# Loads on two queues and four tiles transposed on TensorE, at the start of a gated attention and SwiGLU kernel

## The chip, the cores and the metric

The kernel runs on one core of a Trainium2 chip. The metric is the device time of one execution in microseconds (us). All runs here are in the undisturbed ("fast") state. The profile calls the engines PE (TensorE), DVE (VectorE), ACT (ScalarE), POOL (GpSimd) and SP (SyncE, which issues most loads).

## The reference

The input x has 2048 tokens of 512 features, in bf16. One branch is a linear attention with 32 heads, the other a SwiGLU block; a sigmoid gate mixes them.

```python
x = A_x                                              # 1 x 2048 x 512
g = sigmoid((x * gate_w).sum(-1, keepdims=True))
q, k, v = split(x @ wqkv)                            # (cut)
pq, pk = phi(q), phi(k)         # phi(t) = where(t > 0, t + 1, exp(t)) + 1e-6
o = pq @ (pk^T v) / (pq . sum(pk) + 1e-6)            # for each head
a = o @ wo
b = (silu(x @ w1) * (x @ w3)) @ w2
return g * a + (1 - g) * b
```

## The kernel before

Only the first 10 us matter here. A tile of x is 128 tokens, and there are 16 of them. The k projection needs each tile transposed (xT, features on partitions) and the weights wk. Tiles 0 and 1 are loaded plainly and transposed on PE through an identity matmul; tiles 2 and 3 and all later ones are transposed by DMA. Everything is loaded through the one queue of the sync engine, in the order written.

```python
nc.scalar.activation(out=pre[:], ..., func=ACT.Exp)        # loads ACT's function table early
dq = nc.sync
dq.dma_start(out=x_sb[:, 0:1, :], in_=x_r[:, 0:1, :])      # x tile 0
for i in range(2):                                         # wk in two halves
    dq.dma_start(out=wk_sb[:, 2*i:2*i+2, :], ...)
dq.dma_start(out=x_sb[:, 1:2, :], in_=x_r[:, 1:2, :])      # x tile 1
dq.dma_start(out=xT[:, :, 2*P:TB], in_=x2d[2*P:TB, :], transpose=True)   # tiles 2, 3
dq.dma_start(out=x_sb[:, 2:TPB, :], in_=x_r[:, 2:TPB, :])
# ... tiles 4 to 15 (a DMA transpose and a plain load for each four), then the other weights

def emit_xT(t):                              # one tile: four transposes, one copy from PSUM
    for kc in range(KC):
        nc.tensor.transpose(out=xTp[:, kc, :], in_=x_sb[:, t, kc*P:(kc+1)*P], identity=ident[:])
    if t in (0, 2): nc.vector.tensor_copy(out=xT_t, in_=xTp[:])
    else:           nc.scalar.activation(out=xT_t, in_=xTp[:], func=ACT.Copy)

emit_warm(6)                                 # matmuls on constants
emit_xT(0)
emit_warm(2)
emit_k_mm(k0[0], 0, 0); emit_k_mm(k0[0], 0, 1)     # k(0), first half of wk
emit_xT(1)
emit_k_mm(k0[0], 0, 2); emit_k_mm(k0[0], 0, 3)     # k(0), second half of wk
emit_k_phi(k0[0], 0)                         # exp on ACT, two operations on DVE
for t in range(1, TPB):                      # k(1), k(2), k(3)
    ...
# then, alternating: "XP" matmuls (x^T phi(k)) of tile u and k(t) for t = 4 to 15
```

In the code P is 128, TB is the 512 tokens of a block of TPB = 4 tiles, and KC = 4 counts the chunks of 128 features. k(t) is the projection of tile t, and k(0,2..3) are the last two of its four matmuls. The order of PE's instructions is the written one. The order on the other engines is chosen by the scheduler.

## Time and profile before

The time is 181.27 us (three runs, 181.25 to 181.48). The profiled execution spans 179.2 us.

| reading | value |
|---|---|
| PE busy | 174.8 us, 98% of the span |
| begin of the XP matmuls in the chain | 9.36 us |
| gap before tile 1's transposes, from the end of the matmul slot before it | 0.52 us |
| gap before k(1), likewise | 0.42 us |

First, the page of before. The line is PE's busy time, its share of the span, and its number of instructions.

```profile
PE 174.8 (98%) x884; PEld 83.7 (47%) x884; DVE 118.0 (66%) x202; ACT 65.8 (37%) x123; POOL 61.4 (34%) x69
```

Second, the table of PE's waits in before: the waiting group, what it waited for, the total in us, how often, the longest. These three lines are the whole table. After the first k tiles PE waits no more, so what matters is when the XP matmuls begin.

```profile
PE warm L159 <- PEq L462: 0.8, 1, 0.8
PE xTp L168 <- DMA x_sb<-in_A_x_dram: 0.4, 1, 0.4
PE k L178 <- ACT xT L175: 0.3, 1, 0.3
```

Third, the chain of waits of before in the first 16 us: start, duration, what.

```profile
2.23 3.24 DMA x_sb<-in_A_x_dram
...
5.51 0.41 PE xTp L168 x4
...
5.95 0.60 ACT xT L175
...
6.60 2.76 PE k L178 x12
9.36 0.86 PE XP L198 x4
```

Tile 1 is issued at 2.23 us, behind wk, and lands at 5.465. Then ACT's copy of its transpose (0.60 us) holds k(1) until 6.60.

Fourth, the timeline of PE in before: start, duration of the group, line, operation, tiles, count.

```profile
0.84 2.72 PE L159 MATMUL warm<-const-bfloat16-1.0 128*128 128x512 bf16 x6 [0.84 <-PEq L462]
3.35 0.63 PE L168 MATMUL xTp<-ident,x_sb 128*128 128x128 bf16 x4
3.78 0.95 PE L159 MATMUL warm<-const-bfloat16-1.0 128*128 128x512 bf16 x2
4.56 0.59 PE L178 MATMUL k<-wk_sb,xT 128*128 128x512 bf16 x2
5.51 0.40 PE L168 MATMUL xTp<-ident,x_sb 128*128 128x128 bf16 x4 [0.35 <-DMA x_sb<-in_A_x_dram]
```

The last matmul of a group shows its whole latency, 0.38 us, while matmuls follow each other every 0.216 us; so the wait "0.35" counts from the modelled end, and the time that PE's slot stood empty is larger: the second k(0) matmul starts at 4.78, its slot ends at 4.99, and the transposes start at 5.51, which is 0.52 us. In the same way the gap before k(1) is 6.60 less 6.18, or 0.42 us.

### The profile page before, as it was taken

To read this page: it belongs to the slowest core of one execution; us is meant where nothing else is said; L and a number is where in the kernel's file an instruction comes from. 1 tells how busy PE (TensorE), PEld (TensorE's weight loads), DVE (VectorE), ACT (ScalarE), POOL (GpSimd) and SP (SyncE) were. 2 spreads that over 40 slices of the span, in tenths; PEclk is the share of its full clock that TensorE was granted. 3 is DMA by queue.
4 is the path that set the end of the run, shared out by engine and by line. 5 is a ranking of instruction groups with operands and counts; after the bars stand their busy time and mean duration, and the time that the engine had idled before them with its cause. 6 is when DMAs were issued, how large, how long until landed. Compare 5 with 4: busy or idle time off the path is not lost.

```text
span 179.2 us, 2463 instructions
## 1 busy us (share of the span) xinstructions
PE 174.8 (98%) x884; PEld 83.7 (47%) x884; DVE 118.0 (66%) x202; ACT 65.8 (37%) x123; POOL 61.4 (34%) x69
## 2 busy tenths in 40 slices
PE   8899999999999999999999999999999999999993
PEld 3344444474444545444445444444545444444463
DVE  1388667897998837398787374977764669776000
ACT  3442322566523334343324343332443323331221
POOL 5177765646453323253003232620032328100000
PEclk9999999999999999999999999999999999999999
DMA  5999999901006011115000101240001013300011
GB/s 165 244 242 239 294 334 398 348 28 26 9 11 110 0 44 33 44 42 104 0 0 4 44 31 42 59 90 5 0 7 54 19 59 67 61 0 0 29 46 45
DMA packets 29340, 15.14 MB, mean 84 GB/s; under 512 B 20656, under 2 KB 28304, under 8 KB 29328
## 3 DMA queue, kind: packets, MB, share of 16 engines
q1 hardware_dynamic: 29328, 14.98, 31.2%
q8 instruction: 7, 0.11, 0.3%
q14 instruction: 5, 0.04, 0.1%
HBM read 8.42 MB, written 2.10 MB: 59 GB/s over the span
## 4 chain that ended last, share of the span: by engine, by line
PE 93%; DVE 2%; DMA 2%; SPq 1%; ACT 0%; issue 0%; DVEq 0%
PE o_ps L344 19%; PE gate_ps L301 18%; PE up_ps L307 18%; PE o_ps L335 8%; PE q_ps L211 8%; PE XP L198 8%; PE k_ps L178 6%; PE r_ps L235 3%; PE o_ps L339 2%; DMA x_sb<-in_A_x_dram 2%; PE k L178 2%; DVE hT L317 1%; DVE gs L314 1%; PE kvT_ps L402 0%; SPq L86 0%; PE W_ps L429 0%
## 5 line engine op out<-in xcount | busy, mean ns | idle before, releaser
L301 PE MATMUL gate_ps<-xT,w_sb 128*128 128x512 bf16 x160 | 41.1, 379 | 0.0
L307 PE MATMUL up_ps<-xT,w_sb 128*128 128x512 bf16 x160 | 41.1, 379 | 0.0
L219 POOL TENSOR_TENSOR qz<-pq,z_sb 128x512 f32<-128x512 bf16 x16 | 18.5, 1162 | 60.2 <-DVE pq L143 58.6
L312 ACT ACTIVATE th<-gate_ps 128x512 bf16<-128x512 f32 x40 | 23.9, 597 | 38.2 <-PE gate_ps L301 37.8
L344 PE MATMUL o_ps<-w_sb,hT 128*128 128x512 bf16 (+2 forms) x180 | 37.5, 355 | 0.0
L314 DVE SCALAR_TENSOR_TENSOR gs<-th,gate_ps 128x512 bf16<-128x512 bf16 x40 | 27.3, 682 | 5.9 <-ACT th L312 5.6
L317 DVE TENSOR_TENSOR hT<-up_ps,gs 128x512 bf16<-128x512 f32 x40 | 27.7, 691 | 3.8
L140 DVE TENSOR_SCALAR phi_m<-phi_e 128x512 bf16<-128x512 bf16 x32 | 14.4, 450 | 23.0 <-ACT phi_e L138 22.9
L344 PEld LDWEIGHTS <-hT 128*128 128x128 bf16 x180 | 16.8, 97 | 17.9
L307 PEld LDWEIGHTS <-w_sb 128*128 128x128 bf16 x160 | 15.6, 98 | 19.0 <-issue 0.2
L301 PEld LDWEIGHTS <-w_sb 128*128 128x128 bf16 x160 | 15.6, 98 | 18.9 <-issue 0.3
L349 ACT ACTIVATE o_out<-o_ps,omg 128x512 bf16<-128x512 f32 (+2 forms) x17 | 11.1, 656 | 30.4 <-PE o_ps L344 30.4
L284 POOL TENSOR_TENSOR pqn<-pq,rden 128x512 bf16<-128x512 bf16 x16 | 16.6, 1056 | 14.1 <-DVE rden L277 11.7
L188 POOL TENSOR_TENSOR pks<-pks,pk_sb 128x512 f32<-128x512 f32 x15 | 17.6, 1173 | 8.9 <-DVE pk_sb L143 8.4
L222 DVE TENSOR_REDUCE den<-qz 128x32 f32<-128x512 f32 x16 | 10.9, 684 | 8.9 <-POOL qz L219 8.8
L335 PE MATMUL o_ps<-W_sb,pqT 128*128 128x512 bf16 (+2 forms) x72 | 16.8, 355 | 0.0
L211 PE MATMUL q_ps<-wq_sb,xT 128*128 128x512 bf16 x64 | 16.3, 379 | 0.0
L198 PE MATMUL XP<-pk_sb,x_sb 128*128 128x512 bf16 x64 | 16.1, 379 | 0.0
L138 ACT ACTIVATE phi_e<-k_ps 128x512 bf16<-128x512 f32 x12 | 7.2, 597 | 15.3 <-PE k_ps L178 15.3
L178 PE MATMUL k_ps<-wk_sb,xT 128*128 128x512 bf16 x48 | 12.3, 379 | 0.0
L138 ACT ACTIVATE phi_e<-q_ps 128x512 bf16<-128x512 f32 x16 | 9.6, 597 | 7.0 <-PE q_ps L211 6.8
L143 DVE SCALAR_TENSOR_TENSOR pq<-q_ps,phi_m 128x512 bf16<-128x512 f32 x16 | 11.1, 691 | 0.5
(59 smaller groups left out, 116.5 us busy)
## 6 DMA issues: line engine op xcount, KB each, us to landing
w_sb<-in_B_w_dram SPq DMA_DIRECT2D x3, 1280.0 KB, 9.6
out_dram<-o_out SPq DMA_DIRECT2D x15, 128.0 KB, 1.9
x_sb<-in_A_x_dram SPq DMA_DIRECT2D x3, 512.0 KB, 4.3
wk_sb<-in_A_wqkv_dram SPq DMA_DIRECT2D x2, 256.0 KB, 3.0
wq_sb<-in_A_wqkv_dram SPq DMA_DIRECT2D x1, 512.0 KB, 4.9
wv_sb<-in_A_wqkv_dram SPq DMA_DIRECT2D x1, 512.0 KB, 6.6
wo_sb<-in_A_wo_dram SPq DMA_DIRECT2D x1, 512.0 KB, 10.5
x_sb<-in_A_x_dram SPq DMA_DIRECT2D x2, 128.0 KB, 2.7
```

The lines of the kernel that those rows point to most:

```text
L178: nc.tensor.matmul(k_ps[:], lhsT=xT[:, kc, t * P : (t + 1) * P], rhs=wk_sb[:, kc, :], start=(kc == 0), stop=(kc == KC - 1),)
L188: nc.gpsimd.tensor_add(pks[:], pks[:], pk_sb[:, t, :])
L198: nc.tensor.matmul(XP_ps[dc][:], lhsT=x_sb[:, t, dc * P : (dc + 1) * P], rhs=pk_sb[:, t, :], start=(t == 0), stop=(t == NT - 1),)
L211: nc.tensor.matmul(q_ps[:], lhsT=xT[:, kc, ts_tok], rhs=wq_sb[:, kc, :], start=(kc == 0), stop=(kc == KC - 1),)
L219: nc.gpsimd.tensor_tensor(out=qz[:], in0=st[tb, "pq"][:, tt, :], in1=z_sb[:], op=ALU.mult)
L301: nc.tensor.matmul(gate_ps[:], lhsT=w1_sb[:, kc, fsl], rhs=xT[:, kc, tok_sl], start=(kc == 0), stop=(kc == KC - 1),)
L307: nc.tensor.matmul(up_ps[:], lhsT=w3_sb[:, kc, fsl], rhs=xT[:, kc, tok_sl], start=(kc == 0), stop=(kc == KC - 1),)
L312: nc.scalar.activation(out=th[:], in_=gate_ps[:], func=ACT.Tanh, scale=0.5)
L314: nc.vector.scalar_tensor_tensor(out=gs[:], in0=th[:], scalar=1.0, in1=gate_ps[:], op0=ALU.add, op1=ALU.mult)
L317: nc.vector.tensor_tensor(out=st[tb, "hT"][:, fc, :], in0=up_ps[:], in1=gs[:], op=ALU.mult)
L335: nc.tensor.matmul(o_ps[:], lhsT=st[tb, "pqT"][:, c, tsl], rhs=W_sb[:, c, a:b], start=(c == 0), stop=False,)
L344: nc.tensor.matmul(o_ps[:], lhsT=st[tb, "hT"][:, fc, tsl], rhs=w2_sb[:, fc, a:b], start=False, stop=(fc == FC - 1),)
```

## The change

The intent is to start k earlier. wk is issued from ACT's queue beside x tile 0 on the sync queue, so tile 1 is not behind it. Tiles 2 and 3 are also transposed on PE, so their DMA transpose is gone. Each transposed tile leaves PSUM in two halves, one by DVE and one by ACT.

```diff
-    pre = consts.tile([1, 1], FP32, name="pre")
-    nc.scalar.activation(out=pre[:], ..., func=ACT.Exp)
     dq.dma_start(out=x_sb[:, 0:1, :], in_=x_r[:, 0:1, :])
     for i in range(2):
         kcs = slice(2 * i, 2 * i + 2)
-        dq.dma_start(out=wk_sb[:, kcs, :], in_=wqkv_r[:, kcs, D : 2 * D])
+        nc.scalar.dma_start(out=wk_sb[:, kcs, :], in_=wqkv_r[:, kcs, D : 2 * D])
     dq.dma_start(out=x_sb[:, 1:2, :], in_=x_r[:, 1:2, :])
-    dq.dma_start(out=xT[:, :, 2 * P : TB], in_=x2d[2 * P : TB, :], transpose=True)
     dq.dma_start(out=x_sb[:, 2:TPB, :], in_=x_r[:, 2:TPB, :])
+    pre = consts.tile([1, 1], FP32, name="pre")
+    nc.scalar.activation(out=pre[:], ..., func=ACT.Exp)
 # ... emit_xT:
-        xTp = psX.tile([P, KC, P], BF16, tag=f"XP{t % 3}", name="xTp")
-        ... four transposes; tiles 0, 2 copied by DVE, the others by ACT
+        for h in range(2):
+            xTp = psX.tile([P, 2, P], BF16, tag=f"XP{(2 * t + h) % 3}", name="xTp")
+            ... two transposes
+            if h == 0: nc.vector.tensor_copy(out=xT_t, in_=xTp[:])
+            else:      nc.scalar.activation(out=xT_t, in_=xTp[:], func=ACT.Copy)
 # ... PE's order:
     emit_k_phi(k0[0], 0)
+    emit_xT(2)
     for t in range(1, TPB):
         ... k(t)
+        if t == 1:
+            emit_xT(3)
```

## The prediction

> **What bounds the kernel.** TensorE. The page's busy table gives PE 174.8 us of a 179.2 us span (98%); the chain of waits is 93% PE. The table of waits has only three PE waits in the whole run: 0.8 us at the start, 0.4 us for x tile 1, and 0.3 us for the ScalarE copy of that tile's transpose. So after the first k tiles PE never waits, and the time is the moment at which the "XP" matmuls begin (9.36 us in the chain) plus a fixed PE-bound rest. The change can only move that moment.
>
> **The start of before (timeline, chain).** Six warm-up matmuls hold PE until 3.35 us; x tile 0 lands earlier, at 2.95. Four transposes, two more warm-ups and the DVE copy (0.42 us) bring k(0) to 4.56. x tile 1 is issued only at 2.23, behind x0 and both halves of wk, and lands at 5.47: PE idles 0.35 us. Transposes at 5.51, then k(0,2..3) at 5.75; the ACT copy (0.60 us) makes PE wait again until 6.60. Twelve matmuls then take 2.76 us.
>
> **Removed.** The DMA transpose of tiles 2 and 3 (1.32 us of issue on the sync queue). Everything behind it there is issued some 2.2 us earlier (1.32 plus wk's two issues, 0.42 and 0.46). The wait for x1: now issued near 1.25, I expect it landed by about 4.5, before PE wants it (4.98). The wait for the 0.60 us ACT copy: two halves on two engines, about 0.27 us on DVE and 0.4 on ACT (estimates: about half of 0.42; between the 0.20 of the 1x1 activation and 0.60).
>
> **Added.** Eight transposes on PE at full clock. Before, four took 5.51 to 5.75, so eight cost about 0.5 us, on the critical path. Four half copies each on DVE and ACT in all, instead of one whole one each. The ACT table load (1.28 us) slides to about 1.7 to 3.0, still before ACT's first copy.
>
> **DMA.** The Trainium skill ("DMA: Bandwidth & Descriptors", Issuing engines are not separate DMA queues) says the queues share the same engines and a second issuer saves only issue time. The DMA row agrees that data soon limits: 0.87 to 1.14 busy from 3 to 6 us. So wk beside x0 may delay x0 by up to 0.35 us (harmless: the warm-ups end at 3.35), and wk's second half, now sharing with tiles 2 and 3, should land near 5.2 to 5.5 and gate k(0,2).
>
> **Sum.** k(0) still starts at 4.56 (warm-ups). x1 transposes at 4.98; k(0,2..3) end near 5.65 to 5.95 (6.18 before). Then xT(2), k(1), xT(3), k(2), k(3): 0.25 + 0.86 + 0.25 + 1.72 = 3.08 us, to 8.75 to 9.05. Gain 0.3 to 0.6 us, if no evacuation stalls PE. The risk is DVE order: if the copy of tile 2 queues behind phi(0) (exp 0.59, then 0.29 and 0.69), and tile 3's behind phi(1), PE stalls about 1.3 us and the change loses 0.7 to 1.0 us. Before's GpSimd timeline shows the scheduler taking ready work out of written order (blockmask memset between the two ident steps), so I think this the less likely case, about one in three.
>
> **Prediction: 180.9 us, range 180.3 to 182.0.** Faster by over 2%: 0.01; within 2%: 0.98; slower by over 2%: 0.01.
>
> **What shows it right.** No PE wait for x1; k(0) still near 4.56; the chain reaching "XP" between 8.7 and 9.1; PE's busy time unchanged or up 0.5 us; nothing new waiting later.
>
> **What makes it wrong.** Half copies behind phi on DVE (PE waits on "xT" near 7 to 9 us); wk or tiles 2 and 3 landing after 6 us; a late table load.

## The result, and the profile after

The changed kernel took 181.20 us (four runs, 180.65 to 181.62) against 181.38 us (four runs, 181.25 to 181.73). The ratio is 0.9985, 95% interval 0.9962 to 1.0009: the same. Here and below a ratio is the mean time of one kernel's fast runs over that of the other's of the same rounds, so it is not quite the ratio of the medians quoted. The changed kernel's four runs lie 1.0 us apart, the others 0.5.

The profiled execution is one of the slower ones (181.62 us, span 179.9). Its page, the same line as before: PE is 1.2 us busier.

```profile
PE 176.0 (98%) x892; PEld 84.7 (47%) x892; DVE 118.9 (66%) x205; ACT 66.7 (37%) x126; POOL 61.2 (34%) x69
```

PE's table of waits after has one line. Both waits that the change aimed at are gone.

```profile
PE warm L158 <- PEq L466: 0.8, 1, 0.8
```

The chain of waits after, first 16 us. It is all PE from the start, yet XP begins 0.47 us later than in the trace of before.

```profile
0.84 2.72 PE warm L158 x6
3.56 0.43 PE xTp L169 x4
3.98 0.85 PE warm L158 x2
4.84 0.85 PE k L179 x2
5.69 0.43 PE xTp L169 x4
6.12 0.68 PE k L179 x2
6.80 0.22 PE xTp L169 x4
7.02 0.86 PE k L179 x4
7.88 0.22 PE xTp L169 x4
8.11 1.73 PE k L179 x8
9.83 0.86 PE XP L199 x4
```

The timeline of PE after shows why. The same two k(0) matmuls take 1.06 us (0.59 before), and the same four transposes of tile 1 take 0.63 us (0.40 before).

```profile
3.78 1.06 PE L158 MATMUL warm<-const-bfloat16-1.0 128*128 128x512 bf16 x2
4.63 1.06 PE L179 MATMUL k<-wk_sb,xT 128*128 128x512 bf16 x2
5.49 0.63 PE L169 MATMUL xTp<-ident,x_sb 128*128 128x128 bf16 x4
5.91 0.88 PE L179 MATMUL k<-wk_sb,xT 128*128 128x512 bf16 x2
6.63 0.39 PE L169 MATMUL xTp<-ident,x_sb 128*128 128x128 bf16 x4
```

PE ran at half its clock until about 6.5 us here, and until about 4.5 us in the trace of before. The traces hold records of the clock that agree with the matmuls' pace: before is released to full clock at 4.49 us, after at 6.49. What PE does up to 4.4 us is the same instruction for instruction, so the change did not cause the later release. The page's row of granted clock does not show any of it: it prints 9 in the first slices of both, because there is no record ahead of the first release. At the start of a kernel the spacing of equal matmuls is the safer reading.

The Trainium skill, "TensorE: Matmul & The Clock Gate" (The HAM clock gate), says that PE starts at half clock, and that a monitor with a free-running window of 3.413 us releases it, at a moment that varies from run to run. These traces agree: in all ten traces of kernels of this length the full clock then lasts 174.08 us, which is 51 windows of 3.413.

The loads did what was expected of them. My reading of the trace's landing records: tile 1 landed at 4.21 us (5.46 before), wk's halves at 3.85 and 4.97 (4.07 and 4.83), tiles 2 and 3 at 5.88.

The two theories taken to the chip:

- A, the clock: the change does gain 0.3 to 0.6 us where the clock is released early; with a late release the wait that it removes was not there, and a kernel that never waits takes on the whole variation of the release.
- B, refill: the eight added transposes, and the landing of tiles 2 and 3, use up what the removed waits gave, and the rest is the noise of the chip.

### The profile page after: what moved, and what is told of

The parts are those of the page before. It is cut to its first block, busy times and chain, and to the rows that moved or that the text cites. A ratio compares the mean times of both kernels' runs of the same rounds, so it can differ in the third digit from the quotient of the medians.

```text
span 179.9 us, 2484 instructions
## 1 busy us (share of the span) xinstructions
PE 176.0 (98%) x892; PEld 84.7 (47%) x892; DVE 118.9 (66%) x205; ACT 66.7 (37%) x126; POOL 61.2 (34%) x69
## 3 DMA queue, kind: packets, MB, share of 16 engines
HBM read 8.42 MB, written 2.10 MB: 58 GB/s over the span
## 4 chain that ended last, share of the span: by engine, by line
PE 96%; DVE 2%; issue 0%; DVEq 0%
PE o_ps L345 19%; PE gate_ps L302 18%; PE up_ps L308 18%; PE XP L199 8%; PE o_ps L336 8%; PE q_ps L212 8%; PE k_ps L179 6%; PE r_ps L236 3%; PE k L179 2%; PE warm L158 2%; PE o_ps L340 2%; DVE hT L318 1%; PE xTp L169 1%; DVE gs L315 1%; PE kvT_ps L406 0%; PE W_ps L433 0%
## 5 line engine op out<-in xcount | busy, mean ns | idle before, releaser
L139 DVE TENSOR_SCALAR phi_m<-phi_e 128x512 bf16<-128x512 bf16 x32 | 14.9, 466 | 19.6 <-ACT phi_e L137 19.6
```

## The experiments

Twelve kernels ran, in four groups, each group on one chip with its own runs of before. The release times below come from the clock records of each trace.

### The change again (e1_again)

No edit.

> The changed kernel once more, for its spread. Theory A (clock): at an equal moment of the PE clock's release the change gains 0.3 to 0.6 us, but that moment differs from run to run (4.49 us in the trace of before, 6.49 in the trace of after), and the changed kernel, which never waits, takes all of that on itself. Then its times spread over about 1 us (180.6 to 181.7), more than those of before, its median is 0.1 to 0.5 us lower, and in its trace XP begins near 8.9 us if the clock is released by 4.6, plus about 0.45 us for each us of later release. Theory B (refill): the eight added transposes and the later arrival of tiles 2 and 3 use up what the removed waits gave; then XP begins near 9.4 to 9.8 us even with an early release, and the median is within 0.1 us of before.

Measured: 181.27 us (180.73 to 181.76, six runs), before 181.45 (181.11 to 181.69), ratio 0.9991 (0.9972 to 1.001). The trace: release at 6.67, XP at 9.92. With 6.49 and 9.83 that gives 0.5 us for each us of later release, as half speed must (expected 0.45), but both traces are late ones.

Each run also lists its span and mean granted clock. A recorded clock under 1.000 means that PE fell back to half clock at least 0.18 us before the end (0.0005 x 2 x 179), and since the full clock lasts 174.08 us, that the release was early: before some 4.7 to 5.7 us, by the span of the run (span less 0.18 less 174.08). The cut is not at the same release for all: a run of 178.9 us counts as early only below 4.64, one of 180.0 below 5.74. This sorts the runs (all groups together; the four runs of before in the first result have no clock on record; the changed kernel's are ten, from the first result and from here):

| | recorded clock under 1.000 (early) | 1.000 (mostly late) |
|---|---|---|
| before, 50 runs | mean 181.41 (14 runs, 181.00 to 181.74) | mean 181.56 (36 runs, 181.07 to 182.05) |
| after, 10 runs | mean 180.81 (4 runs, 180.65 to 181.03) | mean 181.50 (6 runs, 180.92 to 181.76) |

After gains 0.60 us where the release was early and 0.06 where it was late. Of before's 50 runs only one (181.00) is faster than the slowest of the four early runs of after (181.03). This is a correlation, over several chips, and the release of a single run is inferred, not seen. On e1_again's chip alone it points the same way, with few runs: early, after 180.87 (3 runs) and before 181.35 (3); late, after 181.66 (3) and before 181.47 (8).

### Only the queue (e2_queue)

```diff
 # before, with
-        dq.dma_start(out=wk_sb[:, kcs, :], ...)
+        nc.scalar.dma_start(out=wk_sb[:, kcs, :], ...)
 # and the table load moved behind it; tiles 2, 3 by DMA transpose, whole copies
```

> Only the DMA half of the change: wk from the ACT queue, table load after it; tiles 2 and 3 still transposed by DMA, whole copies. Theory A: x tile 1 is no longer waited for, the wait for the 0.60 us ACT copy stays (0.2 to 0.4 us); XP begins 0.3 to 0.6 us before where before's does at the same release of the clock; median 0.2 to 0.6 us below before. Theory B: the same or better than that, and clearly (0.3 us or more) below the full change, which pays 0.5 us for transposes.

Measured: 180.62 us (180.45 to 181.29), ratio 0.9961 (0.9944 to 0.9978), on the same chip as e1_again. The queue alone gains 0.39%, 0.7 us (0.4 to 1.0 by the interval), some four times what the whole change did there. Its trace had its release at 5.18 and XP at 9.18; tile 1 is no longer waited for, and the wait for ACT's copy stays (PE's only wait beside the 0.8 us at the start):

```profile
PE k L178 <- ACT xT L175: 0.3, 1, 0.3
```

So theory B's part is needed: the other half of the change costs something. The difference of the two ratios, 0.9991 less 0.9961, is 0.5 us.

### Only the PE half (e3_pe)

```diff
 # after, with
-        nc.scalar.dma_start(out=wk_sb[:, kcs, :], ...)
+        dq.dma_start(out=wk_sb[:, kcs, :], ...)
 # and the table load back in front
```

> Only the PE half: all four tiles transposed on PE in halves, wk still on the sync queue ahead of x tile 1. x tile 1 lands near 5.4 us as before and PE waits for it if the clock is early; tiles 2 and 3 land near 6.2. Theory A: XP at 9.1 to 9.4 with an early clock (9.36 in before), median within 0.2 us of before. Theory B: the transposes are pure cost here, median 0.1 to 0.4 us above before.

Measured: 182.13 us (181.92 to 182.26), ratio 1.0037 (1.0025 to 1.0049): slower by 0.67 us, more than either theory said. PE's wait in the trace:

```profile
PE xTp L169 <- DMA x_sb<-in_A_x_dram: 0.7, 1, 0.7
```

The plain load of tiles 2 and 3 was issued at 2.74 and landed at 7.05, 4.3 us later, not at 6.2. Such a load took 4.2 us after as well; there it is issued at 1.72. So the PE half needs the queue half: alone, it makes PE wait for data that it did not need in that form before.

### Whole copies (e4_whole)

```diff
 # after, with the emit_xT of before:
-        for h in range(2): ... two transposes; h == 0 copied by DVE, h == 1 by ACT
+        ... four transposes
+        if t in (0, 2): nc.vector.tensor_copy(out=xT_t, in_=xTp[:])
+        else:           nc.scalar.activation(out=xT_t, in_=xTp[:], func=ACT.Copy)
```

> The full change, but each tile's transpose copied whole by one engine (DVE for 0 and 2, ACT for 1 and 3). Both theories: the halves are worth nothing where other work of PE stands between a transpose and its use: the second warm-up pair covers tile 0, the k(0) matmuls and tile 2's transposes cover tile 1, k(1) covers tile 2. Median within 0.15 us of the full change; at most one wait of PE for xT, under 0.2 us, before k(3). If the halves matter, PE waits 0.2 us or more for xT and the median rises by that much.

Measured: 181.76 us (181.42 to 181.93), ratio 1.0016 (1.0004 to 1.0028), which is 0.45 us above the change with halves (1.0016 less 0.9991). My expectation failed: the halves are worth it. The timeline of e4_whole, the two weight loads that wait and ACT's lines before the second:

```profile
6.67 0.55 PEld L177 LDWEIGHTS <-xT 128*128 128x128 bf16 x4 [0.20 <-ACT xT L174]
7.74 0.60 ACT L137 ACTIVATE phi_e<-k 128x512 bf16<-128x512 f32 x1 [0.64 <-PE k L177]
8.24 0.59 ACT L174 ACTIVATE xT<-xTp 128x512 bf16<-128x512 bf16 x1
8.88 0.55 PEld L177 LDWEIGHTS <-xT 128*128 128x128 bf16 x4 [0.58 <-ACT xT L174]
```

PE loses time at two places, 0.20 us before k(1), where it waits for ACT's whole copy of tile 1 (the transposes ahead end at 6.47), and 0.25 us before k(3), whose slot was free at 8.63: the whole copy of tile 3 queues behind the exp of k(1) on ACT. Together these are the 0.45 us. I had looked for the danger on DVE; it is on ACT. In after the half copies of tile 3 come late too (DVE 8.40, ACT 8.41), but ACT's takes 0.38 us and not 0.59, and is done at 8.79, just ahead of k(3) at 8.81.

### Behind a lead-in: first try (p_before, p_after)

```diff
 # in both kernels, ahead of the loads
+    wa = psX.tile([P, TB], FP32, tag="XP3", name="wa")
+    for i in range(20):
+        nc.tensor.matmul(wa[:], lhsT=warm_l, rhs=warm_r, start=True, stop=True)
+    nc.vector.tensor_copy(out=x_sb[:, :, 0], in_=wa[:, 0:NT])     # so the loads of x_sb wait
+    nc.vector.tensor_copy(out=wk_sb[:, :, 0], in_=wa[:, 0:KC])    # and of wk_sb, xT, ... (cut)
-    emit_warm(6)  ...  emit_warm(2)
+    emit_warm(13) ...  emit_warm(4)
```

> The kernel before with the moment of the clock's release taken out of it: 20 extra full-width warm-up matmuls run first, and the first loads may only be issued when they are done (a small DVE copy from their PSUM tile into each loaded tile makes the DMA wait), so PE is at full clock from the first transpose on; 13 and 4 warm-ups then cover what 6 and 2 at half clock did. About 8 us longer than before. Theory A (clock): its times agree within 0.3 us, since only the release moved them; XP begins about 8.5 us after the first x load is issued, as in the early-clock trace of before (9.36 less 0.80). Theory B (refill, chip noise): the spread stays at 0.6 us.

> The changed kernel with the same lead-in. Theory A: it is 0.3 to 0.6 us faster than the before-kernel with the lead-in, and its times agree within 0.3 us instead of spreading over 1.0. Theory B: the two are within 0.15 us of each other, or the spread stays at 1 us.

Measured: p_before 188.06 us (187.30 to 188.54), p_after 188.84 (188.11 to 189.24). The totals can't be used, and the fault is in the design: the 20 matmuls themselves last until the release allows, 5.82 us in the one trace and 7.30 in the other, so the variation that was to be removed sits in the lead-in. Within the traces, counted from the issue of the first load, XP came 8.65 us later in p_before (15.59 less 6.94) and 9.03 in p_after (17.45 less 8.42). p_after missed its expectation because wk's second half landed 4.87 us after its issue and PE waited 1.1 us for it:

```profile
PE k L189 <- DMA wk_sb<-in_A_wqkv_dram: 1.1, 1, 1.1
```

With wk on the second queue its landing is less sure: over all traces the second half landed 3.0 to 3.2 us after its issue on the one queue (five traces), and 3.7 to 5.2 on the two (nine). Why it was so late in this run stays open.

The pair shows more than its totals. In p_before PE is at full clock through the whole k stage, and the gap before tile 1 is 0.88 us (the slot of k(0)'s second matmul ends at 10.86), wider than in the first trace:

```profile
11.74 0.40 PE L178 MATMUL xTp<-ident,x_sb 128*128 128x128 bf16 x4 [0.72 <-DMA x_sb<-in_A_x_dram]
```

Part of that is the design: with the 13 and 4 warm-ups k(0) ends 0.28 us sooner after the first load than in before. In p_after the gap is gone. But even without the wait for wk, tiles 2 and 3, which landed at 13.99, would have held XP to about 17.1 (an estimate, with the 3.08 us of work behind them), 8.7 us after the first load and level with p_before: there the loads, not PE, bound the changed kernel.

### Behind a lead-in of fixed length (q_before, q_after)

```diff
 # in both kernels, ahead of the loads; 24 warm-ups run beside this and end early
+    for i in range(14):                                            # each 0.70 us
+        nc.vector.scalar_tensor_tensor(out=scr[:], in0=scr[:], scalar=1.0, in1=scr[:],
+                                       op0=ALU.mult, op1=ALU.mult)
+    nc.vector.tensor_copy(out=gt[:], in_=scr[:, 0:P])              # the later warm-ups wait for gt
+    nc.vector.tensor_copy(out=x_sb[:, :, 0], in_=scr[:, 0:NT])     # the loads, as above (cut)
-    emit_warm(6)  ...  emit_warm(2)
+    emit_warm(12) ...  emit_warm(4)
```

> The kernel before behind a lead-in of fixed length: a chain of 14 DVE operations (about 9 us) holds back the loads, while PE runs 24 warm-up matmuls, which end well after any release of the clock; PE then waits for the DVE chain, and 12 and 4 warm-ups at full clock stand for the 6 and 2 at half clock. The release can no longer touch the k tiles. Theory A (clock): its times spread by no more than those of the unmodified kernel (0.5 us); XP begins 8.5 to 8.7 us after the first x load is issued.

> The changed kernel behind the same fixed lead-in. Theory A: the spread of 1 us falls to under 0.5, and it is 0.3 to 0.6 us faster than the before-kernel with this lead-in (XP 8.0 to 8.3 us after the first load). If wk's second half lands later than about 4 us after its issue, as in the first lead-in (4.87), PE waits for it and the gain shrinks by as much; that would be the DMA's part, not the clock's. Theory B: the two within 0.15 us, and the 1 us spread still there.

Measured, on one chip: q_before 193.43 us (193.31 to 194.33, five runs), q_after 193.56 (192.69 to 194.45, six runs); ratios to the unmodified kernel 1.0663 and 1.0661. They are the same, and q_after still spreads by 1.8 us. Both of theory A's numbers failed. The run list fits the spread: the recorded clock is 0.982 (two half-clock windows of 3.41 us, by 0.5 x 6.8 of 192) in the slowest run of each kernel, 1.000 (none) in q_after's fastest, and 0.991 (one) in the other four of each. Those four lie at 193.31 to 193.60 for q_before (mean 193.44) and at 193.53 to 193.60 for q_after (193.56). So with the clock alike the changed kernel's spread is 0.07 us: here its spread follows the clock, as theory A had it, but the gain isn't there. (The windows are inferred from each run's mean clock; two runs were traced.) The traces tell why. The stretches of q_before (start:end and length; busy time of PE, PEld, which is PE's weight loads, DVE, ACT and POOL with instruction counts; granted clock, DMA share, GB/s):

```profile
9.60:13.00 3.40, 0.91 (x5) 0.43 (x6) 3.19 (x16) 0.00 (x0) 0.00 (x0) 1.00 0.00 0
13.00:16.40 3.40, 3.40 (x10) 1.20 (x9) 0.00 (x0) 0.00 (x0) 0.00 (x0) 0.50 0.82 245
```

PE's wait of 3.3 us for the DVE chain was enough for the clock to fall back, from 13.00 to 16.42 us. So the 12 warm-ups took 4.5 us in place of 2.6, and the loads had landed when PE wanted them. The release (16.42 and 16.53) came just ahead of the k tiles in both. By accident this is a clean measurement of one thing: the k stage at full clock with all loads in time. PE's timeline in q_before:

```profile
18.13 0.59 PE L197 MATMUL k<-wk_sb,xT 128*128 128x512 bf16 x2
18.98 2.76 PE L197 MATMUL k<-wk_sb,xT 128*128 128x512 bf16 x12 [0.26 <-ACT xT L194]
21.59 1.03 PE L217 MATMUL XP<-pk_sb,x_sb 128*128 128x512 bf16 x4
```

and in q_after:

```profile
18.13 0.59 PE L198 MATMUL k<-wk_sb,xT 128*128 128x512 bf16 x2
18.56 0.39 PE L188 MATMUL xTp<-ident,x_sb 128*128 128x128 bf16 x4
18.79 1.03 PE L198 MATMUL k<-wk_sb,xT 128*128 128x512 bf16 x4
19.65 0.39 PE L188 MATMUL xTp<-ident,x_sb 128*128 128x128 bf16 x4
19.87 1.89 PE L198 MATMUL k<-wk_sb,xT 128*128 128x512 bf16 x8
21.60 1.03 PE L218 MATMUL XP<-pk_sb,x_sb 128*128 128x512 bf16 x4
```

The two are level at 18.13 us and level at XP, 21.59 and 21.60. The gap before k(1) that before still has, 0.42 us (18.98 less the slot's end at 18.56), is what the eight transposes take: the k matmuls start 0.23 and 0.22 us after the transposes ahead of them. The second removed gap is given back in full. What is left to gain is the gap before tile 1, and it was not there in these two.

### Before again (e6_before)

No edit: the kernel before against itself.

> The kernel before, unchanged, timed against itself, for one more trace of its start and for the noise of such a comparison. By now the account is: with an early release of the clock the change gains the gap before x tile 1 (about 0.5 us from matmul to matmul); with a late one PE, at half clock, reaches that point only when the tile has landed, and nothing is gained, since the other gap (0.43 us) is given back by the eight transposes (0.43). So if this trace shows a release at 5.5 us or later, PE's gap before x tile 1's transposes is under 0.15 us, no wait for the tile is listed, and XP begins at 9.7 to 10.0; if the release comes by 4.6 it looks like the first trace (gap 0.52, XP 9.36). Its times do not depend on the release by more than 0.3 us. Ratio to itself within 0.1%.

Measured: 181.29 us (181.07 to 182.05) against 181.67 (181.00 to 182.02), ratio 0.9989 (0.9967 to 1.0011). A kernel differs from itself by as much as the change did. The trace has a late release, at 6.00 us. The chain:

```profile
2.23 3.57 DMA x_sb<-in_A_x_dram
...
5.84 0.47 PE xTp L168 x4
...
6.99 2.76 PE k L178 x12
9.75 0.86 PE XP L198 x4
```

XP begins at 9.75, as expected. The gap before tile 1's transposes did shrink, but to 0.35 us (the slot of k(0)'s second matmul ends at 4.64 plus two times 0.43, or 5.49), and not under 0.15, because tile 1 landed later than in the first trace, at 5.79 and not 5.46. Against tile 1's landing of the first trace it would have been nothing. PE's table of waits lists none for it.

So before's XP begins at 9.36 for a release at 4.49 and at 9.75 for 6.00, 0.39 us later. But 0.33 of that is tile 1's later landing; only 0.06 is the clock's, in tile 1's transposes (0.47 against 0.41 in the chains). Where before waits for the tile, as in both traces, the landing sets its start, and the release hardly matters. After pays 0.5 us per us of later release, as it has no wait to absorb it in. Carried back at 0.5 per us, after's XP would begin at 9.58 for a release at 6.00 (0.17 us ahead of this trace of before, but 0.16 behind it had tile 1 landed as in the first, 9.36 plus 0.06), and at 8.83 for 4.49 (0.53 ahead; nearer 8.96 if tiles 2 and 3 gate, 5.88 plus the 3.08 us of work behind them). These are estimates from the traces; no trace of after with an early release was caught.

### Combining the parts (e5_mix, b_mix, b_swap)

```diff
 # e5_mix: e2_queue with the halves of the change (tiles 2, 3 stay with the DMA transpose)
 # b_mix:  e5_mix with
-    emit_warm(2)
+    emit_warm(1)
 # b_swap: b_mix with
-    dq.dma_start(out=x_sb[:, 2:TPB, :], in_=x_r[:, 2:TPB, :])
     for tb in range(1, NTB):
         dq.dma_start(out=xT[:, :, tb * TB : (tb + 1) * TB], ..., transpose=True)
+        if tb == 1:
+            dq.dma_start(out=x_sb[:, 2:TPB, :], in_=x_r[:, 2:TPB, :])
```

> Queue half of the change plus halves: wk from the ACT queue, tiles 0 and 1 evacuated in halves by two engines, tiles 2 and 3 still by DMA transpose. Both theories: the 0.3 us wait for the whole ACT copy in the queue-only kernel goes, no transposes are added, so it is 0.1 to 0.3 us below the queue-only kernel (180.62) and 0.5 to 1.0 below before, unless the DMA-transposed tiles 2 and 3 land after PE wants k(2) (about 7.3 us); then PE waits for xT there.

> The same with one warm-up matmul in place of two between the first transposes and k(0), since a half copy (0.29 us) is done before one half-clock matmul (0.43 us) ends. Theory A: PE's work before XP falls by 0.43 us at half clock and by about 0.3 with an early release; median 0.2 to 0.45 below the kernel with two, if the release does not come later. If the missing work delays the release or x tile 1 (4.2 us) or wk's second half (5.0) gates instead, the gain is under 0.1 us.

> The one-warm-up kernel, with the plain load of tiles 2 and 3 (wanted only by the XP matmuls, after 10 us) moved behind the DMA transpose of tiles 4 to 7, for which k(4) waited until 9.22 us in the trace of the one-warm-up kernel. That transpose is issued 0.6 us earlier; if its landing follows, the wait (about 0.5 us) goes and the median falls by 0.2 to 0.5 us against that kernel (180.88), to below 180.6. If the DMA engines and not the order set the landing, nothing changes.

Measured: e5_mix 180.58 us (180.25 to 181.02), ratio 0.9949 (0.9935 to 0.9962). b_mix 180.88 (180.40 to 181.01), ratio 0.9959 (0.9946 to 0.9972). b_swap, in the next group, 180.40 (180.25 to 181.00), ratio 0.9939 (0.9921 to 0.9957). All three beat before by 0.7 to 1.1 us, and their ratios lie below the changed kernel's in e1_again, though on other chips. They are not told apart from each other. e5_mix differs from the changed kernel in one thing only, tiles 2 and 3 by DMA transpose in place of eight transposes on PE, so it prices that part of the change: 0.9949 against 0.9985 and 0.9991, or 0.65 to 0.76 us, across chips, give or take some 0.4 by the two intervals together.

In e5_mix PE waits for nothing after the start and XP begins at 8.86 for a release at 5.39. b_mix gains nothing by its missing warm-up: its release came at 3.69, its k stage was early, and then k(4) had to wait for the DMA transpose of tiles 4 to 7, landed at 9.22. b_swap removed that wait, and in its place PE waited 0.2 us each for tile 1 and for wk's second half. In this trace the loads bound the start.

## Why the prediction was right or wrong

- **The time: right.** 180.9 was predicted, 181.20 measured, inside 180.3 to 182.0. But with a kernel differing from itself by 0.11% the time is no strong test, and luck had a part: XP missed its range by 0.7 us or more in both traces, and a range of 1.7 us held that too. The parts are the test.
- **PE bounds the kernel, and only the start can move: right.** From XP to the last matmul both kernels take the same 166.9 to 167.1 us. In both traces of after, and in the late one of before, a small gap of 0.13 to 0.2 us appears near 30 us, where the XP matmuls of one tile wait for DVE by the look of it (in after DVE's last operation on pk_sb ends at 30.47, the next weight load starts at 30.52); the first trace of before doesn't have it. It is not the change's own.
- **No PE wait for tile 1, and its landing by 4.5: right** (4.21). **wk's second half near 5.2 to 5.5:** it landed at 4.97 and gated nothing in after, though it did in p_after and b_swap.
- **k(0) at 4.56, k(0) done by 5.65 to 5.95, XP at 8.7 to 9.1: wrong in the traces.** XP began at 9.83 and 9.92. The step that failed is "k(0) still starts at 4.56 ... k(0,2..3) end near 5.65 to 5.95": I took the clock of the one trace for a property of the kernel. In after's traces PE was at half clock until 6.49 and 6.67, and this stretch took twice as long.
- **Eight transposes cost about 0.5 us: near right.** At full clock they cost 0.44 to 0.45 us and, as q_before and q_after show, exactly return the removed gap before k(1).
- **"Gain 0.3 to 0.6 us": half right.** It rests on the gap before tile 1 (0.52 us in the first trace). The runs sorted by recorded clock gain 0.60 us with an early release and 0.06 with a late one; most executions are late. The mean gain is 0.27 us in the first result and 0.16 in e1_again, neither clear of noise.
- **The DVE order as the risk: the order came out as hoped, the place was wrong.** DVE took tile 2's half copy (6.95) ahead of phi(0) (7.46) and tile 3's (8.40) ahead of phi(1) (8.59). e4_whole shows that the copy that PE ends up waiting for is ACT's, and that the halves are short enough to avoid it.
- **PE's busy time up 0.5 us: it rose 1.2.** That the rest is the longer half clock is likely, but was not worked out.

Where the expected gain went, then: the queue half earns 0.7 us; the PE half spends about 0.5 of it, in transposes that the DMA did at no cost to PE. That the queue's gain comes from tile 1's gap is shown by e2_queue's waits; its size, 0.7 with an interval of 0.4 to 1.0, lies above the 0.52 and 0.35 us of the gap in the two traces of before, and that difference is not explained. That this gap depends on the clock is shown in part: by the runs sorted by clock, and by the gap itself, 0.88 us at full clock throughout (p_before, in part by its shorter warm-up), 0.52 with a release at 4.49 and 0.35 at 6.00, where the tile landed later too. The experiments that were to isolate the clock gave no clean gain: in p_after the loads were late, in q_before the gap was not there.

The Trainium skill, "DMA: Bandwidth & Descriptors" (Issuing engines are not separate DMA queues), says that a second issuing engine saves only issue time. These traces agree for the most part: tile 1 was issued 0.97 us earlier (1.25 against 2.23), and landed 1.25 us earlier (4.21 against 5.46 in the traces of after and before). The other 0.28 us is a shorter time from issue to landing (2.96 against 3.24). That 512 KB of wk no longer stood ahead of it in its queue may be the reason, but no run isolates that, and in b_swap, also on two queues, the time was 3.62.

## What to carry to other kernels

Take a change with two halves apart before judging it: here one half gains 0.4% and the other gives most of it back. Work moved to the engine that bounds the kernel (the transposes) costs its full time there, even when it removes a wait; a load moved to a second queue out of the way of the first wanted tile was the only gain that is clear of noise. In the first microseconds, read PE's clock from the spacing of equal matmuls, in more than one trace, before costing anything from durations there.

## What the Trainium skill lacked or had wrong

- "TensorE: Matmul & The Clock Gate" warns of PE idle gaps above about 3.4 us. Here a wait of 3.3 us, of which some 2.5 us fell into the window that ended at 13.0, dropped the clock to half for 3.4 us (q_before and q_after, both traces); a wait of 1.1 us did not (p_after).
- The same page gives about 3.4 us of sustained work until the release. PE began at 0.84 us and was released between 3.69 us (b_mix, 2.85 us later) and 6.67 (e1_again, 5.83 us later). Counted back from the release in windows of 3.413 us, b_mix's window began at 0.28, so PE was busy for some 83% of it, while e1_again's earlier window ended at 3.26 after 71% and brought no release.
- The same page says that the cost of the ramp is under 1% of a typical kernel, and not to fit to a count of slow matmuls. Here its variation alone is 0.4%, as large as the effect studied: 0.7 us between early and late runs of a kernel that never waits at its start, and 0.15 us for one that does (by the sorted runs).
- "DMA: Bandwidth & Descriptors" gives no figure for what a second queue does to the landing of single loads: here tile 1 landed 1.25 us earlier, at the cost of a later and less sure landing of wk's second half (3.0 to 3.2 us after its issue on one queue, 3.7 to 5.2 on two).
- No page says that a profile's row of granted clock can show full clock before the first release; here it did until 4.49 and 6.49 us.
